# One table of order and one of buffer numbers, made anew for a kernel that mixes a spectral filter and an MLP

## The chip, the cores and the metric

The kernel runs on one core of a Trainium2 chip. The metric is device time in microseconds (us), the median of three runs; less is better. The core has a matrix engine (PE, whose weight loads are shown apart as PEld), a vector engine (DVE), an activation engine (ACT), a general engine (POOL), and SP, which here only issues DMAs. Each engine works through its own row of instructions in order; semaphores tell one engine what another has finished, and also tell an engine of its own results.

## The reference

Two branches are computed from one 2048 x 512 input and mixed by a gate, all in float32:

```python
g = sigmoid((x * gate_w).sum(-1, keepdims=True))
a = irfft2(rfft2(x) * (w_r + 1j * w_i))        # x: 2048 x 512, w: 2048 x 257
b = gelu(x @ w1 + b1) @ w2 + b2                # w1: 512 x 1792, w2: 1792 x 512
out = g * a + (1 - g) * b
```

Both branches read the same x; it reaches the kernel in two layouts, xt and xc.

## The kernel before

The 2048 rows are 16 blocks of 128, numbered j. Matrix products at full precision are made of three products of rounded parts (high x high, high x low, low x high); the parts are made by ACT (the high one, a rounding copy) and by DVE (the low one, a subtraction). Where DVE is to be spared, ACT writes the negated high part and POOL adds the source to it with an accumulating DMA (`acc`, L412).

The spectral branch has four stages. `forward` (L585 on) transforms one block: sums and differences of x (eo, w), products with a cosine table (pd), rounding into zb (L628 by ACT, L632 by DVE), products with a table tf (py), and results in y. `stage1` and `filt` are radix-4 butterflies on DVE (`radix4`, L680 to L688, the products with the filter wf at L775 to L779). `stage4` and `inverse` (L825 on) go back: turned rows sw and pq, products pz with a table tg, rounding into zb (L852 by ACT, L853 by DVE), products pa with ci, sums w, and an accumulating DMA that adds the other branch.

The MLP is worked by groups of hidden features. `seven` makes products of a 2 x 2 block scheme with seven products instead of eight (nuA, uxA, nuB, uxB); `plain` does the first group directly (ph); `gelu` (L919) is applied in place, and `split` makes the parts g_h and g_l (L429 and L476). `down` multiplies with w2: ACT loads the running sum s into a PSUM bank po (L968), PE adds, and ACT copies it back into s (L429). The last group goes through `down_seven` (dx, dm, dn, dz, dl), whose results are the output.

All these steps are collected in a graph of 2146 numbered steps. Nothing plans at build time: `ORDER` (L126) lists all the steps in the order in which they are emitted, and `SLOTS` (L212) gives, for each buffer in the order of first use, its number in a pool: 7 buffers of 2 KB per partition (t2k), 3 tables (ttab), 8 for rounded x (xhl), 46 working buffers (w) and the 8 PSUM banks (ps). Each engine's row is the part of `ORDER` that is its own; SP and POOL issue their DMAs in that order too. A buffer is taken over by another tile when the last reader of the former has been emitted:

```python
last = held.get((b.tag, b.slot))
assert last is b or last is None or last.left == 0
assert last is b or not b.onto or last.full
held[b.tag, b.slot] = b
```

The first step that writes a buffer taken over waits, by semaphore, for the last steps that used it. Where that last step is of the same engine, the engine waits for its own result; so it does where an operation reads, or writes over, what the operation ahead of it on its engine has made or read. PE's matmuls are all issued at L420, so they are told apart by the names of their tiles.

Of the kernel before, what the change touches and what calls it, by code (L numbers as in the profile page):

```python
# [126 lines left out]
0 2 8 15 12 108 6 9 489 1 31 32 60 18 7 19 20 28 27 30 22 21 16 17 490 59 491 13 14 10 29 23 496 62 107 55 3 56 24 58  # L127
497 498 25 36 4 38 86 85 57 64 11 114 63 492 37 40 66 65 39 499 35 46 81 82 111 110 72 84 192 113 42 43 47 112 67 5
500 41 70 68 69 44 197 198 48 199 73 119 219 225 45 200 49 120 83 90 138 224 71 143 145 227 226 118 74 121 144 146 165
123 171 173 170 172 50 51 75 115 87 139 127 91 76 508 124 166 493 549 494 495 167 77 92 94 122 125 516 248 672 520 33  # L130
61 89 626 140 169 168 517 518 566 93 128 512 116 521 129 130 548 126 580 174 96 97 117 501 522 88 34 98 502 175 509
176 513 510 628 95 131 99 132 177 221 142 504 178 179 52 53 100 519 141 503 148 530 133 511 180 78 101 514 181 582 523
147 150 80 505 183 539 54 193 581 152 506 182 220 515 102 194 222 195 103 184 149 542 583 223 540 156 507 565 564 543
527 153 151 185 186 157 154 585 552 196 629 365 595 201 271 541 892 229 202 187 531 544 528 135 249 250 568 550 366
251 553 203 367 252 231 204 188 545 554 584 158 159 532 155 206 524 189 191 571 207 536 569 160 575 546 210 104 587
630 570 106 233 529 230 79 161 205 105 588 586 556 272 525 234 228 547 589 208 232 576 591 572 211 134 235 212 537 538
573 533 590 592 551 676 209 555 254 236 273 275 627 256 602 526 1458 342 274 557 567 294 684 648 258 633 259 561 558
162 634 237 559 534 238 574 317 319 213 604 607 631 650 593 642 594 369 318 632 239 278 214 535 562 608 240 215 635
636 577 276 277 279 677 653 281 609 637 654 603 680 241 253 282 638 560 606 295 644 285 280 598 655 656 782 610 578
685 242 652 673 286 737 388 647 255 368 611 613 296 596 939 411 283 639 287 284 243 678 322 563 321 190 288 679 640  # L140
612 605 257 674 675 686 657 289 649 299 597 260 290 262 614 615 579 320 261 298 618 658 164 263 297 291 622 681 651
616 323 619 343 344 346 645 264 345 617 412 216 265 682 620 683 659 293 687 300 664 623 325 621 266 624 625 660 700
163 267 327 706 668 669 302 670 701 301 328 707 304 245 454 389 390 392 347 303 305 331 665 306 292 661 413 671 307
218 702 391 414 453 662 708 136 600 324 326 244 703 308 456 663 415 329 330 332 348 709 309 704 333 601 334 350 217
710 372 352 694 353 335 310 311 695 705 356 599 312 688 689 374 377 336 784 268 270 785 349 741 351 643 137 455 458
357 459 783 378 337 457 371 358 460 945 789 373 354 690 355 790 313 247 246 646 666 667 787 696 788 793 359 691 394
269 791 724 375 376 338 462 360 361 370 395 697 794 461 692 725 417 379 792 397 400 464 396 398 399 467 416 736 738
698 711 401 468 938 828 726 718 719 380 693 727 393 803 720 893 712 463 743 1462 314 419 465 713 402 425 339 721 739
421 699 730 897 731 795 422 466 315 381 316 426 418 403 362 742 744 745 943 382 740 747 748 786 404 420 714 427 899
900 722 383 405 901 423 894 384 364 732 428 340 801 1459 751 406 715 728 898 903 746 424 385 471 363 407 799 757 836  # L150
386 387 729 436 341 429 430 753 408 410 904 944 1078 485 832 448 431 433 1119 733 758 432 409 723 905 760 798 469 434
734 797 752 478 804 472 477 435 829 806 902 946 470 475 476 735 474 830 759 749 716 762 717 767 809 810 833 763 755
800 449 480 959 840 26 450 764 808 813 765 750 479 486 1463 482 831 768 481 796 473 483 484 487 761 949 774 814 837
834 950 811 838 1084 906 984 641 488 775 1464 776 812 777 895 805 778 1079 766 835 807 820 815 816 779 862 856 1065
1067 769 850 839 824 857 780 1085 781 770 863 851 1064 1109 1107 858 1110 864 852 1070 841 842 821 1066 844 845 825
826 822 827 896 865 843 771 772 823 773 988 846 1071 1069 853 859 817 818 874 875 847 914 860 866 985 916 1105 1087
907 1068 1106 1086 1088 1112 1108 754 908 1432 910 1089 1111 1113 1114 1159 802 1115 819 1116 861 1120 1121 848 919
1122 1123 1124 437 867 947 918 1081 948 886 868 1080 1117 854 1154 1152 109 992 756 1155 1153 880 849 1082 1118 855
869 881 876 923 940 989 990 913 1072 912 887 986 1520 996 993 941 1436 1156 1157 915 917 888 924 925 877 889 870 1434
1433 920 994 1073 1437 911 1090 909 997 930 1083 934 1158 921 926 1125 1669 1126 1127 1164 922 927 928 1165 1128 1091  # L160
929 931 935 932 878 998 942 890 882 960 871 936 1161 1092 937 991 987 951 962 1465 995 883 879 1438 1016 1024 891 872
1129 1093 873 1094 1439 1130 1074 1460 1546 954 965 952 1075 964 884 1017 1451 1440 1442 957 1461 1166 1184 961 1160
438 969 1178 953 1467 966 885 1032 1452 967 1162 1025 1466 968 963 970 1441 976 1163 1201 1202 1477 1478 1000 1167
1026 971 972 933 977 1472 1185 1168 1169 1095 1487 1076 439 1170 973 1179 1181 1180 974 1008 1001 1516 1515 1018 980
981 982 983 1077 1019 1002 1182 1171 1453 999 1468 1187 1479 1033 1009 1027 975 1448 1131 1003 1056 1443 1010 1048
1004 1020 1005 1207 1186 1473 1188 1480 978 1205 1484 1668 958 1040 1132 1189 1519 1550 1057 1011 1134 1133 1021 1034
1028 1029 1199 1200 1183 1049 1135 1203 1012 1469 979 1481 1225 1226 1449 1486 1470 1517 1435 1711 1213 1137 1444 1013
1446 1670 1041 1058 1050 1489 1518 1059 1204 1208 1042 1136 1210 1551 1552 1209 1447 1671 1214 1206 1216 1490 1051
1522 1138 1485 1215 1139 1524 1474 1445 1492 1043 1052 1053 1673 1140 1227 1141 1142 1471 1527 1450 1143 1211 1228
1674 1229 1212 1217 1547 1548 1035 1491 1060 1493 1475 1488 1172 1061 1675 1147 1676 1454 1528 1529 1530 1521 1044  # L170
1482 1045 1230 1219 1554 1144 1145 1036 1037 1526 1523 1218 1150 1455 1677 1495 1678 1679 1220 1222 1680 1531 1231
1232 1500 1525 1496 1533 1497 1456 1681 1494 1498 1502 1146 1534 1535 1151 1476 1503 1221 1173 1536 1504 1505 1712
1532 1499 1537 1538 1234 1672 1683 1685 1501 1684 1549 1553 1507 1223 1682 1457 1483 1713 1555 1294 1558 1539 1540
1688 1506 1508 1689 1509 1690 1687 1541 1511 1542 1233 1149 1692 1693 1512 1513 1148 1174 1543 1175 1096 1587 1691
1235 1236 1556 1514 1099 1694 1686 1707 1699 1592 442 1708 1559 1700 1597 1176 440 1703 1544 1701 1560 443 1557 1224
1510 1177 1100 1190 1237 1194 1192 1702 1695 1598 1704 1567 1593 1705 1709 1696 1577 1545 1191 1706 1568 1714 1561
1594 1599 1569 1588 1582 441 1697 1562 1600 1601 1197 1198 1710 1698 1743 1583 1097 1572 446 1563 1815 1193 1102 1195
1196 1589 1241 1564 1570 1571 1814 1239 1101 1253 1238 1240 1244 1243 1098 1245 1844 1573 447 1246 1247 1248 1584 1879
1242 1325 1103 1254 1595 1578 1596 1574 1739 1565 1579 1719 1744 1566 1880 1715 1881 1590 1249 1591 1735 1585 1816 444
1580 1740 1104 1250 1252 1326 1251 1258 1883 1581 1586 1731 1716 1745 1255 445 1845 955 1575 1736 1717 1884 1323 1257  # L180
1256 1259 1305 1720 1746 1718 1727 1732 1737 1721 1851 1576 1723 1327 1722 1738 1885 1329 1324 1022 1850 1818 1813
1817 1342 1404 1054 1328 1343 1846 1260 1265 1330 1335 451 1062 1336 1046 1261 1887 1966 1063 1332 1262 1875 1331 1733
1728 1006 1741 1742 1333 1263 1853 1724 1353 1820 1297 1822 1014 1400 1334 1276 1401 1405 1888 1847 1402 1729 1730
1268 1030 1856 1876 1857 1403 1824 1829 1409 1407 1819 1858 1725 1825 1821 1264 1877 1406 956 1859 1940 1849 1337 1848
# [1198 lines left out]
```

## Time and profile before

| | |
|---|---|
| median of 3 runs | 358.88 us (358.22 to 358.91) |
| the profiled execution | 358.41 us |
| its span, first to last instruction | 356.6 us |
| mean granted TensorE clock | 0.996 |
| DMA moved | 74.63 MB, mean 209 GB/s |
| chain that ended last, by engine | PE 62%, ACT 17%, DVE 15%, issue 4% |

The span is cut into rows by stage, and each row gives busy time and the number of instructions by engine. Times within the span count from its start. Matmuls are pipelined and their ends are modelled, so PE is best read by how fast one start follows another. A "chain of waits" is followed back from the last instruction: at each step to what released it, or to the instruction ahead of it on its engine. In a row of a timeline the first number is the start, the second the duration (records of one engine overlap), and what stands in brackets is idle time and what ended it.

### The profile page before, as it was taken

The numbers are of one execution on the slowest core, as the hardware profiler recorded it, in microseconds if no ns is written. First come the engines' busy times: TensorE is split into PE (matmuls) and PEld (weight loads), VectorE is DVE, ScalarE is ACT, GpSimd is POOL, SyncE is SP. The second block draws the span as 40 slices with busy tenths as digits, with TensorE's granted clock in tenths as the row PEclk, the third lists the DMA queues.
The fourth block names the chain that finished last, engine by engine and source line by source line (L and its number), as shares of the span: only waits on it lengthen the run. The fifth ranks groups of instructions, "written<-read, shape, count | busy, mean of one in ns | idle before, by whom it ended". The sixth has DMA issues, their size and how long they took to land.

```text
span 356.6 us, 5786 instructions
## 1 busy us (share of the span) xinstructions
PE 348.4 (98%) x1742; PEld 291.6 (82%) x1742; DVE 336.6 (94%) x700; ACT 303.5 (85%) x631; POOL 56.8 (16%) x75
## 2 busy tenths in 40 slices
PE   8999999999999999999999999999999999999894
PEld 7988888888887888888888888887878888888773
DVE  5999999999899999999999999999999999999991
ACT  3999999999999958996968983888999999999632
POOL 1011001100112003020213030000200000443520
PEclk9999999999999999999999999999999999999998
DMA  7999949863899699799899655856755629499996
GB/s 205 389 247 266 361 133 295 199 194 112 254 300 187 114 345 272 157 277 269 267 274 195 167 78 125 283 194 205 153 134 148 210 74 251 68 170 211 162 219 204
DMA packets 47719, 74.63 MB, mean 209 GB/s; under 512 B 5544, under 2 KB 18344, under 8 KB 47688
## 3 DMA queue, kind: packets, MB, share of 16 engines
q1 hardware_dynamic: 37528, 58.42, 50.1%
q0 software_dynamic: 9728, 15.51, 27.5%
q10 hardware_dynamic: 432, 0.33, 0.3%
q8 instruction: 14, 0.23, 0.3%
q14 instruction: 17, 0.14, 0.1%
HBM read 52.02 MB, written 17.31 MB: 194 GB/s over the span
## 4 chain that ended last, share of the span: by engine, by line
PE 62%; ACT 17%; DVE 15%; issue 4%; DVEq 0%; ACTq 0%
PE po L420 21%; PE uxB L420 7%; PE uxA L420 6%; PE nuB L420 5%; PE nuA L420 5%; PE ph L420 4%; PE pd L420 3%; PE dx L420 3%; PE py L420 3%; ACT sw L836 2%; PE pa L420 2%; DVE y L682 1%; DVE y L680 1%; PE none L420 1%; PE pz L420 1%
## 5 line engine op out<-in xcount | busy, mean ns | idle before, releaser
L968 ACT ACTIVATE po<-s 128x512 f32<-128x512 f32 x40 | 23.6, 601 | 4.2 <-DVE g_12l L476 1.7
L429 ACT ACTIVATE s<-po 128x512 f32<-128x512 f32 x40 | 22.9, 591 | 1.7 <-PE po L420 1.5
L836 ACT ACTIVATE sw<-y,keep 64x512 f32<-64x512 f32 x32 | 22.7, 719 | 1.6 <-DVE y L684 1.0
L775 DVE TENSOR_TENSOR m<-y,wf 128x514 f32<-128x514 f32 x32 | 21.3, 690 | 0.7
L420 PE MATMUL py<-zb,tf 128*128 128x258 f32 x96 | 20.9, 300 | 0.1
L420 PEld LDWEIGHTS pz<-tg,pq 128*128 128x128 f32 x128 | 17.5, 190 | 1.7 <-DVE pq L840 0.3
L420 PE MATMUL pz<-tg,pq 128*128 128x128 f32 x128 | 18.8, 275 | 0.0
L420 PEld LDWEIGHTS py<-zb,tf 128*128 128x128 f32 x96 | 16.0, 189 | 3.2 <-ACT pys L648 0.6
L420 PE MATMUL pa<-zb,ci 128*128 128x256 f32 x96 | 17.1, 292 | 1.5 <-DVE zb L853 1.0
L420 PE MATMUL pd<-cf,w 128*128 128x129 f32 x128 | 18.6, 275 | 0.0
L420 PEld LDWEIGHTS pa<-zb,ci 128*128 128x128 f32 x96 | 14.4, 188 | 4.9 <-ACT od L429 1.7
L420 PEld LDWEIGHTS pd<-cf,w 128*128 128x128 f32 x128 | 17.4, 190 | 1.1
L420 PE MATMUL nuB<-xB,wB0h 128*128 128x512 f32 x56 | 17.5, 393 | 0.0
L978 ACT ACTIVATE s<-po,b2t 128x512 f32<-128x512 f32 x16 | 10.8, 694 | 6.9 <-PE po L420 6.7
L420 PE MATMUL nuA<-xA,wA0h 128*128 128x512 f32 x48 | 15.0, 393 | 0.0
L632 DVE TENSOR_TENSOR zb<-pd,zb 128x256 fp32r<-128x256 f32 x32 | 13.3, 419 | 1.5 <-ACT logit L631 1.4
L593 DVE TENSOR_TENSOR eo<-xf 128x256 f32<-128x256 f32 x32 | 12.7, 417 | 1.2 <-DMA xf<-in_x0g 1.0
L652 ACT ACTIVATE y<-pys 64x257 f32<-64x257 f32 x32 | 13.2, 416 | 0.6
L840 DVE TENSOR_TENSOR pq<-y,sw 128x256 f32<-128x256 f32 x32 | 13.1, 417 | 0.4 <-ACT sw L836 0.3
L414 POOL DMA_DIRECT2D wA0l<-in_w x6 | 5.1, 898 | 52.4 <-DVE wsA L1188 23.8
L596 DVE TENSOR_TENSOR w<-eo 128x256 f32<-128x256 f32 x32 | 12.8, 419 | 0.3
L414 POOL DMA_DIRECT2D w<-bacc x8 | 10.9, 1369 | 9.3 <-DVE w L881 3.4
(595 smaller groups left out, 1270.5 us busy)
## 6 DMA issues: line engine op xcount, KB each, us to landing
wf<-in_wf SPq DMA_DIRECT2D x16, 257.0 KB
xf<-in_xt SPq DMA_DIRECT2D x14, 256.0 KB
tf<-tf SPq DMA_DIRECT2D x16, 192.0 KB
wrA<-in_w SPq DMA_DIRECT2D x12, 256.0 KB
xbA<-in_xc SPq DMA_DIRECT2D x8, 256.0 KB
xbB<-in_xc SPq DMA_DIRECT2D x8, 256.0 KB
bacc<-s SPq DMA_DIRECT2D x8, 256.0 KB
w<-bacc POOLq DMA_DIRECT2D x8, 256.0 KB, 4.9
```

The costliest lines, as they stand in the source:

```text
L414: return add("pool", 0.92, 3.3, lambda: nc.gpsimd.dma_start(dst(), src(), accum_op=ALU.add), reads, writes, 2.2 * kb / 350)
L420: pe.matmul(ps, w, x, start=start, stop=stop, **more)
L429: a(lambda: act.activation(o.ap(), i.ap(), AF.Copy, scale=scale), n, [i], [o])
L593: v(lambda s=s, op=op: vec.tensor_tensor(eo.ap()[:, s], x.ap()[:, 0:2], x.ap()[:, 2:4], op=op), 256, [x], [(eo, s)])
L596: v(lambda s=s, op=op: vec.tensor_tensor(w.ap()[:, s], eo.ap()[:, :, 0], eo.ap()[:, :, 1], op=op), 256, [eo], [(w, s)])
L632: v(lambda c=c: vec.tensor_tensor(segs(xl, c), both(c), segs(xh, c), op=ALU.subtract), 256, [ps[c], (xh, c)], [(xl, c)])
L652: a(lambda o=o, i=i: act.activation(Y[j].ap()[o:o + HP, 1], pys.ap()[i:i + HP, 1], AF.Copy), 257, [(pys, 1)], [(Y[j], 1 + k)], more=0.07)
L775: v(lambda mk=mk, k=k, y=y, w=w: vec.tensor_tensor(mk.ap(), y.ap(), w.ap()[:, k:k + 1, :ND].to_broadcast([P, 2, ND]), op=ALU.mult), 514, [ ...
L836: a(lambda sw=sw, y=y, o=o, i=i: act.activation(sw.ap()[o:o + HP], y.ap()[i:i + HP], AF.Copy, scale=keep.ap()[i:i + HP]), 512, [y, keep, * ...
L840: v(lambda sw=sw, pq_=pq_, y=y, k=k, op=op: vec.tensor_tensor(pq_.ap()[:, k], y.ap()[:, k], sw.ap()[:, 1 - k], op=op), 256, [y, TURNED[c], ...
L968: a(lambda ps=ps, n=n, o=o: act.activation(ps.ap(), o.ap()[:, n], AF.Copy), size, [o], [ps], more=0.04)
L978: a(lambda o=o, ps=ps, q=q: act.activation(o.ap(), ps.ap(), AF.Identity, bias=b2t.ap()[:, q:q + 1]), 600, [b2t, ps], [o])
```

## The change

`ORDER` and `SLOTS` are replaced by new lists of the same 2146 steps and of the same buffers. The planner that made the new ones, which is not part of the kernel, counts an engine's wait for its own last result where it takes over a buffer from its preceding operation. No other line changes; the pools keep their sizes. The first lines of both tables:

```diff
 ORDER = """
-0 2 8 15 12 108 6 9 489 1 31 32 60 18 7 19 20 28 27 30 22 21 16 17 490 59 491 13 14 10 29 23 496 62 107 55 3 56 24 58
+0 2 3 19 16 8 9 6 489 496 1 32 31 34 27 12 28 21 20 7 22 490 29 23 30 14 18 15 17 4 56 55 24 60 58 13 57 497 498 25 36
...
 SLOTS = """
-0 0 0 1 2 6 8 0 0 0 0 0 0 4 0 1 1 2 3 0 6 1 0 0 7 0 4 5 7 2 0 10 1 2 0 0 5 0 0 0 1 7 2 4 3 5 4 34 13 0 6 2 3 2 5 7 0 0
+0 0 0 1 2 6 9 0 0 0 0 0 0 4 1 0 0 2 3 0 6 1 0 1 5 1 4 5 4 0 1 0 2 7 2 0 3 0 0 0 0 5 0 5 3 4 2 14 12 2 12 2 3 1 5 3 6 1
...
```

What it moves is shown at three places. The first is DVE's row some 55 rows ahead of its end, in the last group of the MLP (g2 and g3 are values behind the gelu, g5f their parts) and the last inverse transform (zb from pz). Before:

```order
L1238 SCALAR_TENSOR_TENSOR g2_11_3919<-gb_2689,uxB50_3599 128x512 [waits DMAHW3_49,Activation_49]
L490 TENSOR_TENSOR g5f3_3930<-g2_10_3735,g5f2_3902 128x512 [waits DMASW0_49,Activation_49]
L1137 TENSOR_TENSOR g2_10_3735<-g3_11_3828,g2_10_3735 128x512 [waits DVE_49]
L853 TENSOR_TENSOR zb1_106<-pz4_3858,zb0_88 128x4x128 [waits PE_49]
L853 TENSOR_TENSOR zb1_106<-pz0_3822,zb0_88 128x4x128 [waits PE_49,Activation_49]
```

and after the change, in the same part of DVE's row:

```order
L490 TENSOR_TENSOR g5f3_3932<-g2_10_3716,g5f2_3903 128x512 [waits DMAHW2_49,PE_49,Activation_49]
L1238 SCALAR_TENSOR_TENSOR g2_12_3934<-gb_2718,nuB60_3865 128x512 [waits DMAHW1_49,Activation_49]
L840 TENSOR_TENSOR pq8_3908<-y_271,sw8_3850 128x256
L993 TENSOR_TENSOR s31_2804<-s31_2804,y_271 128x512
L853 TENSOR_TENSOR zb1_87<-pz4_3862,zb0_89 128x4x128
L1137 TENSOR_TENSOR g2_10_3716<-g3_11_3831,g2_10_3716 128x512 [waits DVE_49]
```

The L1137 row writes over g2_10, which the L490 row reads. It stood right behind L490; now four rows lie between them, so that the result it waits for is five rows old.

The second place is PE's row at the last inverse transform (pz feeds zb, pa reads zb; dx, dm and uxB are products of the MLP's last group, po of `down`). Before:

```order
L420 MATMUL pz12_3997<-tg01_3577,pq12_3881 128x128 x2
L420 MATMUL pz8_3981<-tg01_3577,pq8_3810 128x128 x2
L420 MATMUL dx1_3990<-gx60_3962,v06_3505 128x512 x3
L420 MATMUL uxB60_3885<-xBt4_2263,wB16_3733 128x512 x6
L420 MATMUL pa01_4052<-zb0_88,ci_3004 128x256 x2
L420 MATMUL pa01_4052<-zb1_106,ci_3004 128x256
```

and after the change:

```order
L420 MATMUL pz12_3990<-tg01_3523,pq12_3798 128x128 x2
L420 MATMUL dx0_4019<-g5f0_3825,v05_3624 128x512
L420 MATMUL dx0_4019<-g5f1_3845,v05_3624 128x512
L420 MATMUL dx0_4019<-g5f0_3825,v05_3624 128x512
L420 MATMUL dm1_4023<-g5f2_3903,vsh5_3657 128x512
L420 MATMUL dm1_4023<-g5f3_3932,vsh5_3657 128x512
L420 MATMUL dm1_4023<-g5f2_3903,vsl5_3755 128x512
L420 MATMUL uxB60_3887<-xBt4_2407,wB16_3518 128x512 x6
L420 MATMUL pa01_4037<-zb0_89,ci_2462 128x256 x2
L420 MATMUL po2_320_3619<-g3_5h_3279,wb5h_2841 128x512
L420 MATMUL po2_320_3619<-g3_5l_3281,wb5h_2841 128x512
L420 MATMUL po2_320_3619<-g3_5h_3279,wb5l_2897 128x512
```

Behind the last row shown three products of dx follow before the first pa that reads zb1, DVE's part. Between the last pz and that pa stood nine products of 512 columns; now there are 18. Further on, the second half of pa01's products, which three products of dx divided from the first, stands behind six products (dx1 and dm0), and three more of dx1 lie inside it.

The third place is the start of SP's row. Before:

```order
L551 DMA b2t<-in_b 128x4
L522 DMA xf_95<-in_xt 128x256
L911 DMA war_97<-in_w 128x256
L522 DMA xf_95<-in_xt 128x256
L911 DMA war_97<-in_w 128x256
```

and after the change:

```order
L522 DMA xf_93<-in_xt 128x256
L911 DMA war_96<-in_w 128x256
L522 DMA xf_93<-in_xt 128x256
L911 DMA war_96<-in_w 128x256
L527 DMA cf<-cf 128x258 x2
```

The load of b2t, the bias of the second layer, was the first of all and stands 23rd now; what stood behind it has moved up by one.

198 rows, old and new, of tables (ORDER, SLOTS) are left out of this document.

## The prediction

> **What bounds the kernel now.** I read the page's busy table first, then the table by stage, then the chain of waits.
>
> ```profile
> PE 348.4 (98%) x1742; PEld 291.6 (82%) x1742; DVE 336.6 (94%) x700; ACT 303.5 (85%) x631; POOL 56.8 (16%) x75
> ```
>
> ```profile
> 20.00:100.00 80.00, 79.86 (x434) 68.07 (x433) 76.01 (x175) 78.75 (x200) 7.96 (x12) 1.00 0.78 225
> 100.00:240.00 140.00, 140.00 (x616) 114.98 (x615) 138.25 (x264) 113.25 (x218) 22.40 (x26) 1.00 0.83 219
> 240.00:330.00 90.00, 89.34 (x491) 75.67 (x490) 87.14 (x180) 86.91 (x151) 16.28 (x18) 1.00 0.66 164
> 330.00:351.30 21.30, 20.27 (x98) 16.36 (x96) 19.29 (x36) 9.97 (x19) 7.47 (x7) 1.00 0.92 206
> ```
>
> In a row by stage the columns are the stage, its length, then busy us (and count) of PE, PEld, DVE, ACT and POOL, the granted clock, the DMA share and GB/s. PE, DVE and ACT all look nearly full, so the share of busy time doesn't decide, and PE's ends are modelled. What decides is how fast PE's matmuls follow each other. The chain of waits shows their price where nothing disturbs them:
>
> ```profile
> 112.32 5.44 PE uxA L420 x24
> ```
>
> ```profile
> 301.99 0.47 PE pa L420 x4
> 302.46 0.89 PE pz L420 x8
> ```
>
> That is 5.44/24 = 0.227 us for 512 columns, 0.47/4 = 0.118 for 256, and 0.89/8 = 0.111 for 128 columns in float32 (two records per matmul). Now each stage can be priced. From 100 to 240 there are 616 matmuls in 140 us, 0.2273 each: PE loses 0.3 us at most. From 240 to 330 the groups by shape are these two, two odd records, and 277 of 512 columns for the rest of the 491:
>
> ```profile
> L420 PE MATMUL pz<-tg,pq 128*128 128x128 f32 x128 | 18.8, 275 | 0.0
> L420 PE MATMUL pa<-zb,ci 128*128 128x256 f32 x84 | 15.0, 291 | 0.5 <-ACT od L429 0.3
> ```
>
> They need 14.3 + 9.9 + 62.8 us, and the stage lasts 90, so 3.1 are lost. From 20 to 100 (255 of 512 columns, 81 of 258, 96 of 129) the same sum leaves 2.0; behind 330 it leaves 1.8, and before 20, beside the 1.1 us until the first matmul, 1.4. **PE's losses are 8.7 us in all** (1.4 + 2.0 + 0.3 + 3.1 + 1.8, rounded). The matmuls, the 1.1 at the head and some 5.3 behind the last matmul stay whatever the order. So an order can win at most 8.7 us, and almost nothing in the middle 140.
>
> **The change, part by part.** It is one table of order and one of buffer numbers; no operation is added or taken away. The sum is made against the profiled execution, 358.41 us (span 356.6 and 1.8 around it), which lies 0.47 under the median of 358.88.
>
> *Term 1: waits for the engine's own last result.* Here are neighbours on DVE, then on ACT, with and without such a wait:
>
> ```profile
> 317.64 0.68 DVE L1238 SCALAR_TENSOR_TENSOR g<-gb,uxB 128x512 f32<-128x512 f32 x1
> 318.24 0.68 DVE L490 TENSOR_TENSOR g5f<-g,g5f 128x512 fp32r<-128x512 f32 x1
> 318.96 0.69 DVE L1137 TENSOR_TENSOR g<-g,g 128x512 f32<-128x512 f32 x1
> ```
>
> ```profile
> 290.30 0.57 ACT L429 ACTIVATE s<-po 128x512 f32<-128x512 f32 x1
> 290.90 0.60 ACT L968 ACTIVATE po<-s 128x512 f32<-128x512 f32 x1
> 291.44 0.55 ACT L429 ACTIVATE uxB<-nuB 128x512 f32<-128x512 f32 x1
> 291.92 0.59 ACT L429 ACTIVATE od<-pa 128x512 f32<-128x512 f32 x1
> ```
>
> The L490 row follows its predecessor after 0.60 us. The L1137 row overwrites g, which L490 has just read, waits for it, and starts 0.72 after it: **the wait costs 0.12 us**. On ACT the copy of po into s is followed by the load of po from s after 0.60, while uxB<-nuB, as large a copy from PSUM without such a wait behind it, is followed after 0.48: again 0.12. Counted over the two orders, rows that wait for the row right ahead fall from 72 to 33 on DVE and from 44 to 31 on ACT. By stage, before and after: DVE 15 and 5 in 20 to 100, 39 and 21 in 100 to 240, 12 and 2 in 240 to 330; ACT 5 and 0, 30 and 21, 7 and 7. (The few others are at the two ends.) What goes in the middle is worth nothing: PE loses nothing there, and DVE, busy for 138.25 of 140 us, is fast enough beside it. In the two stages where PE does lose time, (10 + 5) x 0.12 = 1.8 us and 10 x 0.12 = 1.2 us go, beside losses of 2.0 and 3.1. Between nothing and all 3.0 can reach PE. I take half, **-1.5**, since the waits for which PE's weight loads stand end with ACT as often as with DVE, and most of what goes is DVE's:
>
> ```profile
> PEld pa L420 <- ACT od L429: 1.7, 4, 0.5
> PEld pa L420 <- DVE zb L853: 1.2, 1, 1.2
> ...
> PEld uxB L420 <- ACT uxB L429: 0.6, 1, 0.6
> PEld py L420 <- ACT pys L648: 0.6, 1, 0.6
> ```
>
> A rule of the Trainium skill speaks against this term: "VectorE: DVE Perf Modes", section "The DRAIN you can't avoid", has eight copies in a row take as long with a semaphore after each as with one behind the last, and says "the semaphore costs nothing extra here". By it term 1 would be 0 and the sum 1.5 us higher. The trace disagrees, with 0.72 beside 0.60.
>
> *Term 2: the last inverse transform.* The longest single loss stands near the end of PE's row:
>
> ```profile
> 328.05 0.89 PE pz L420 x8
> 328.94 0.70 PE dx L420 x3
> 329.64 1.40 PE uxB L420 x6
> 331.04 0.04 DVEq L490
> 331.07 1.16 DVE zb L853 x2
> 332.23 0.04 issue
> 332.27 0.74 PE pa L420 x4
> 333.02 0.69 PE dx L420 x3
> 333.71 0.98 PE pa L420 x6
> ```
>
> ```profile
> 329.53 1.07 ACT L852 ACTIVATE zb<-pz 128x512 fp32r<-128x512 f32 x2
> ```
>
> After the last pz at 328.94 ACT must round two blocks into zb and DVE must form two remainders, which end near 332.2. PE has only dx, uxB and two of pa in between, 0.70 + 1.40 + 0.24 us, so it could go on at 331.25 and goes on at 332.27: 1.0 us lost. The next six pa take 0.98 where 6 x 0.118 = 0.71 would do: 0.27 more. In the new order dx, dm, six uxB, two of pa, three of po and three of dx stand there, 18 x 0.227 + 0.24 = 4.3 us instead of 2.3, and six matmuls, 1.4 us, divide the second half of pa, where three did. DVE's two zb keep their place, 32 rows ahead of its last. The cover exceeds the lateness twice over, so I take all of it, **-1.3**; it is 0 only if DVE itself gets 2 us later against PE, and term 1 makes it earlier.
>
> *Term 3: the head.* b2t, not needed before the first sums are evicted, leaves the first place in SP's row; the loads behind it are issued one place earlier.
>
> ```profile
> 0.75 0.39 SPq L551 DMA_DIRECT2D b2t<-in_b  x1
> 1.20 0.42 SPq L522 DMA_DIRECT2D xf<-in_xt  x1
> ```
>
> ```profile
> 5.14 1.06 PE L420 MATMUL ph<-xf,war 128*128 128x128 f32 x4
> 5.96 0.37 PE L420 MATMUL none<-zero 128*128 128x256 f32 x1
> 6.27 1.58 PE L420 MATMUL ph<-xf,war 128*128 128x128 f32 x12
> ```
>
> The four ph records at 5.14 need 0.45 us and the next real ones start at 6.27, with the second half of war, so up to 0.45 us (1.20 - 0.75) can be won. The transfers share their engines, and xf of ACT's queue now has an earlier rival: it may win nothing or lose as much. I take **-0.2**.
>
> *Term 4: new places.* Every matmul has new neighbours, and some result will come late where none did. The longest of the waits for ACT quoted above are 0.5 and 0.6 us in one piece, the 1.7 us of pa are four of 0.4 on average; between none and four such may appear. I take two small ones, **+0.7**; the largest gap of before, the 1.0 of term 2, bounds a single one.
>
> Sum: -1.5 - 1.3 - 0.2 + 0.7 = -2.3, so 356.1 on the profiled execution's scale. Set half-way from its scale to the median's, that is **356.3 us**.
>
> **Rivals.**
>
> *1: the freed time isn't PE's.* DVE and ACT start earlier and then wait for what PE makes. For it: PE waits for a single result at each place, and an engine that is ahead gains nothing. Against it: DVE and ACT are busy for 76.01 and 78.75 of 80 us, then 87.14 and 86.91 of 90, just where PE loses. Term 1 is then 0: 356.3 + 1.5 = 357.8. (The rule of the Trainium skill weighed under term 1, from "VectorE: DVE Perf Modes", would give the same time; the spacing of 0.72 speaks against it, and it adds nothing to this chance.)
>
> *2: slower, by the first group's accumulated halves.* The low halves of wA go through POOL, in order, once ACT has written their negated copies:
>
> ```profile
> 29.50 0.84 POOL L414 DMA_DIRECT2D wA0l<-in_w  x1 [7.83 <-ACT zb L628]
> ```
>
> ```profile
> wA0l<-in_w POOLq DMA_DIRECT2D x6, 256.0 KB, 5.8
> ```
>
> ```profile
> 41.53 0.39 PE L420 MATMUL nuA<-xA,wA0l 128*128 128x512 f32 x1
> ```
>
> Issued at 29.50 and landed some 5.8 us later, this half has 6.2 us in hand before nuA reads it at 41.53. In the new order ACT makes that copy 2.7 us of its own work later and PE comes to the matmul 0.8 us of its work earlier: 2.7 are left. ACT is the fullest engine of that stage (78.75 of 80 us), so lateness there isn't made up. It decides as soon as the copy comes over 2.7 us later than the order implies. One that misses by as much as POOL waited for ACT at this very place, 7.83, costs 7.83 - 2.7 = 5.1 us, and DVE and ACT behind it don't win it back: 356.3 + 5.1 = 361.4; a miss of half that gives 357.5. Against it: the raw blocks from which these halves are made stand earlier in SP's row, 18th and 19th rather than 27th and 30th.
>
> That the table doesn't do what it says can be left out, since the counts of waits above are of the two programs.
>
> **How the numbers follow.** Forecast 0.58, its own range 354.0 to 358.0 (term 1 whole and no term 4 give 353.9; term 1 at a quarter and term 4 doubled give 358.1). Rival 1 has 0.20, rival 2 0.22. A measurement of this kernel tells 0.2%, 0.72 us, from no change, so faster is below 358.16. The forecast lies there but for 0.02, and of rival 1, at 357.8, some 0.12: with 0.01 of rival 2, **0.68 faster**. Of rival 1 0.06, of rival 2 0.05 and of the forecast 0.02 are the same: **0.13**. Slower: 0.16 of rival 2, 0.02 of rival 1 and 0.01 of the forecast, **0.19**. The range is 354.0 to 359.8, which leaves out the lower edge of the forecast and some 0.15 of rival 2.
>
> **What would show it.** The spacing of DVE's rows should be 0.60 at the places named, with few of 0.72, and DVE's busy share lower by about 1%. PE's row should show pa without a gap at the last inverse, and some 490 matmuls in less than 90 us in the stage from 240 on. The first real ph should stand before 6.2. Rival 1 would show DVE and ACT idle more, with PE's losses as before; rival 2 a pause of over 1 us in PE's row before the first nuA, ended by a DMA. A loss of over 1 us at any place that I don't name would break term 4, and with it the forecast.

## The result and the profile after

The changed kernel takes **353.64 us** (353.41 to 353.74, 4 runs) beside 358.89 for the kernel before: ratio 0.9854, 95% interval 0.9837 to 0.9871, or 5.2 us. 356.3 was forecast, with 354.0 as the lower end: the direction was right, the size half of what came. The profiled execution took 353.74 us, its span is 352.0.

The busy table of the changed kernel, and its table by stage (columns as in the prediction):

```profile
PE 344.8 (98%) x1742; PEld 291.9 (83%) x1742; DVE 333.4 (95%) x700; ACT 301.6 (86%) x631; POOL 56.6 (16%) x75
```

```profile
20.00:100.00 80.00, 79.98 (x435) 68.36 (x435) 77.01 (x176) 78.71 (x202) 7.97 (x12) 1.00 0.78 228
100.00:240.00 140.00, 140.00 (x618) 115.28 (x617) 137.55 (x267) 113.21 (x219) 22.44 (x26) 1.00 0.83 223
240.00:330.00 90.00, 90.00 (x504) 78.21 (x503) 88.56 (x184) 87.74 (x155) 19.40 (x20) 1.00 0.68 160
330.00:351.30 21.30, 16.38 (x80) 13.51 (x78) 14.15 (x26) 6.95 (x14) 4.12 (x4) 0.97 0.87 218
```

Shares of busy time say almost nothing here; counts do. From 240 to 330 PE now runs 504 matmuls instead of 491. The chain of waits, which gave PE 62% before, is PE's own row:

```profile
PE 96%; DVE 1%; DMA 1%; issue 0%; ACT 0%; DVEq 0%
```

PE's losses, worked out as in the prediction (start to start, less 0.227, 0.1175 or 0.1115 us by shape), and of them the waits longer than 0.095 us in one piece (each cell and each sum rounded by itself):

| stage | loss before | loss after | long waits before | after |
|---|---|---|---|---|
| 0 to 20 | 1.4 | 1.1 | 1.2 | 1.0 |
| 20 to 100 | 2.0 | 1.5 | 0.9 | 0.3 |
| 100 to 240 | 0.4 | 0.1 | 0.2 | 0.1 |
| 240 to 330 | 3.1 | 0.9 | 2.1 | 0 |
| from 330 | 1.8 | 0.1 | 1.7 | 0 |
| sum | 8.6 | 3.7 | 6.0 | 1.4 |

PE loses 4.9 us less, and 4.7 of that are long waits that are gone, 3.7 of them behind 240. In the list of what PE's weight loads wait for, the stage from 240 to 330 has seven rows before and none after. The last inverse transform in PE's row of the changed kernel, and DVE's two zb that it needs:

```profile
326.18 0.40 PE L420 MATMUL pa<-zb,ci 128*128 128x256 f32 x2
326.42 0.40 PE L420 MATMUL po<-g_5h,wb5h 128*128 128x512 f32 x1
...
327.12 0.85 PE L420 MATMUL dx<-gx,v 128*128 128x512 f32 x3
327.81 0.63 PE L420 MATMUL pa<-zb,ci 128*128 128x256 f32 x4
```

```profile
325.38 1.28 DVE L853 TENSOR_TENSOR zb<-pz,zb 128x512 fp32r<-128x512 f32 x2
```

The zb end at 326.66, 1.15 us ahead of the pa that reads them; none of these rows of PE has idle time in brackets. And DVE's row in the last group; before, L1137 started 0.72 behind the row whose result it waited for:

```profile
318.63 0.70 DVE L1231 TENSOR_TENSOR uxB<-uxB,fiveB 128x512 f32<-128x512 f32 x1 [0.29 <-PE uxB L420]
319.24 0.68 DVE L1137 TENSOR_TENSOR g<-g,g 128x512 f32<-128x512 f32 x1
319.84 0.68 DVE L490 TENSOR_TENSOR gx<-g,gx 128x512 fp32r<-128x512 f32 x1
320.44 0.68 DVE L1238 SCALAR_TENSOR_TENSOR g<-gb,uxB 128x512 f32<-128x512 f32 x1
```

Every start follows the last by 0.60 or 0.61, and DVE now waits for PE.

### The profile page after: what moved, and what is told of

The parts are those of the page before. It is cut to its first block, busy times and chain, and to the rows that moved or that the text cites. A ratio compares the mean times of both kernels' runs of the same rounds, so it can differ in the third digit from the quotient of the medians.

```text
span 352.0 us, 5796 instructions
## 1 busy us (share of the span) xinstructions
PE 344.8 (98%) x1742; PEld 291.9 (83%) x1742; DVE 333.4 (95%) x700; ACT 301.6 (86%) x631; POOL 56.6 (16%) x75
## 4 chain that ended last, share of the span: by engine, by line
PE 96%; DVE 1%; DMA 1%; issue 0%; ACT 0%; DVEq 0%
PE po L420 37%; PE uxB L420 11%; PE uxA L420 9%; PE nuB L420 8%; PE nuA L420 7%; PE pd L420 4%; PE pz L420 4%; PE py L420 3%; PE pa L420 3%; PE ph L420 3%; PE dx L420 3%; DMA xf<-in_x0g 1%; PE dm L420 1%; PE dn L420 1%; PE dz L420 1%; DVE eo L593 0%
## 5 line engine op out<-in xcount | busy, mean ns | idle before, releaser
L628 ACT ACTIVATE zb<-pd 128x256 fp32r<-128x256 f32 x32 | 12.1, 392 | 0.4 <-PE pd L420 0.4
L420 PEld LDWEIGHTS nuB<-xB,wB0h 128*128 128x128 f32 x56 | 10.4, 188 | 2.0
```

What stands on the lines that cost most here:

```text
L420: pe.matmul(ps, w, x, start=start, stop=stop, **more)
L628: a(lambda c=c: act.activation(segs(xh, c), both(c), AF.Copy), 256, [ps[c]], [(xh, c)])
```

## The experiments

Two things changed at once: how often DVE and ACT wait for their own last result (72 to 33 rows on DVE, 44 to 31 on ACT), and the order. Buffer numbers alone move the first without the second. Each run was compared with runs of the kernel before on the same chip (358.1 to 358.5 there). Where a table was set in other lines, L851 stands for L853 and so on.

### Buffer numbers alone

`s_all` and `s_mid`: before's order, new numbers. Of 900 numbers 374 and 175 differ; the first of s_all:

```diff
 SLOTS = """
...
-34 13 0 6 2 3 2 5 7 0 0 14
+23 13 0 6 2 3 2 5 7 0 1 14
...
```

> The kernel before with its own order of steps, row for row, and buffer numbers changed alone: two numbers change places wherever a step of DVE or ACT would take over a buffer from the step right ahead of it. Rows that wait for the row right ahead fall from 72 to 33 on DVE and from 44 to 33 on ACT, nearly the counts of the changed kernel (33 and 31). Theory 'own waits, by stage' (term 1 of the prediction): 10 + 4 such waits of 0.12 us go in each of the two stages where PE loses or fewer, half of them reach PE: about -1.1 us, 357.8. Theory 'own waits, carried': also the 20 + 7 that go between 100 and 240 count, since DVE and ACT come out of that stage earlier and PE's later losses (3.1 us behind 240) shrink: -2.5 us or more, 356.4 or less. Theory 'order': buffer numbers alone win nothing, 358.7 or more.

> As the run before this one, but the buffer numbers change places only where DVE's row stands between 100 and 240 us: there DVE's waits for the row right ahead fall from 39 to 19, ACT's from 30 to 23, elsewhere nothing changes. Theory 'own waits, by stage': 0, since PE loses nothing in that stage, 358.9. Theory 'own waits, carried': -1 us or more, 357.9 or less, and PE's losses shrink behind 240, not before. Theory 'order': 358.9.

Measured: 366.09 (ratio 1.0235, 1.0197 to 1.0274) and 367.83 (1.0261, 1.0233 to 1.0288). No theory had this. The timelines of ACT and DVE of s_mid show why:

```profile
147.02 0.60 ACT L429 ACTIVATE g_10h<-nuA 128x512 fp32r<-128x512 f32 x1 [4.35 <-DMA su<-wAsh]
149.07 0.21 ACT L772 ACTIVATE wf<-edges 128x4 f32<-128x4 f32 x1 [1.46 <-DMA wf<-in_wf]
```

```profile
149.31 0.70 DVE L775 TENSOR_TENSOR m<-y,wf 128x514 f32<-128x514 f32 x1 [5.38 <-ACT wf L772]
```

g_10h had been given a buffer that a store (su<-wAsh) was still reading, and ACT stood for 4.35 us. In s_all the same wait took 6.9 us. A number that saves 0.12 us on DVE can cost some 36 times that at a DMA, or more. These two runs say nothing of the waits themselves.

`a_all` and `a_mid`: the changed kernel's order, with own waits put back by buffer numbers (357 and 207 differ; no stall by a DMA came with them).

```diff
 SLOTS = """
...
-1 0 1 5 1 4 5 4 0 1 0 2 7 2
+0 0 0 5 1 4 5 4 1 0 0 2 7 2
...
```

> The changed kernel with its own order of steps, row for row, and buffer numbers changed alone, so that DVE and ACT again take over buffers from the step right ahead: waits for the row right ahead rise from 33 to 72 on DVE (as before the change) and from 31 to 41 on ACT. Theory 'own waits, by stage': 10 + 0 come back in 20 to 100 and 7 + 2 in 240 to 330, half of 2.3 us reaches PE: 354.8. Theory 'own waits, carried': +2.5 us or more, 356.1 or more. Theory 'order': at most +0.3, 353.9.

> As the run before this one, but only between 100 and 240 us: DVE's waits for the row right ahead rise from 22 to 38 there, ACT's from 21 to 29. Theory 'own waits, by stage': 353.6, no change against the changed kernel. Theory 'own waits, carried': 354.6 or more, with the new losses behind 240. Theory 'order': 353.6.

Measured: **354.45** (0.9888, 0.9873 to 0.9903) and **353.52** (0.9862, 0.9843 to 0.9880). 39 waits on DVE and 10 on ACT, 5.9 us of their rows, cost 0.8 us by the medians and 1.2 by the ratios; the 16 and 8 in the middle cost nothing. Compared row by row with the changed kernel, DVE in a_mid is up to 1.3 us late, at 200, and 0.4 at 240, while PE's row keeps its times from 60 us to the end. In this order the theory "carried" falls, and with a_all it is seen that the order alone, with as many own waits on DVE as before, brings 4.1 of the 5.2 us.

`s2_all`, `s4`, `s4_mid`: before's order again, with numbers that touch no load or store soon before or after.

> The kernel before with its own order and buffer numbers changed alone, as in s_all, but two numbers change places only where the buffer that is given up isn't taken by a load or an accumulating DMA within the next 120 steps, nor by another engine within 20. Rows that wait for the row right ahead fall from 72 to 38 on DVE and from 44 to 38 on ACT. If s_all was slower by what its buffers did to loads, this one isn't. Theory 'own waits, by stage': half of (6 + 4 + 4) x 0.12 us, -0.8, 358.1. Theory 'own waits, carried' or 'DVE's lag': DVE reaches 331 some 4 us of its own work earlier and the gap there closes, -1.2 to -2.5, 356.4 to 357.7. Theory 'order': 358.6 or above.

Measured: 357.41 (0.9972, 0.9953 to 0.9992), with two waits of DVE for DMAs left, 2.1 and 2.0 us, at 63 and 119. The next two are free of them (174 and 165 numbers differ):

```diff
 SLOTS = """
...
-5 32 24 41 0 0 0 3 2 1
+5 32 24 36 0 0 0 3 2 1
...
```

> The kernel before with its own order and buffer numbers changed alone, behind 100 us only, and only where the buffer given up isn't wanted by a load within 300 steps, and the one taken was last used by no DMA within 200: so free of the two stalls by DMAs (2.0 us each) that s2_all had. Waits for the row right ahead: 47 instead of 72 on DVE, 38 instead of 44 on ACT. Theory 'DVE's lag': 25 x 0.12 = 3.0 us less on DVE's row, of which PE gets back 2 or more: 356.5 or less. Theory 'own waits, by stage' (term 1): half of (3 + 4) x 0.12, -0.4, 358.0. Theory 'places': 358.4.

> As s4, but only where DVE's row stands between 100 and 240 us: 19 waits fewer there on DVE, 2 on ACT, 2.3 us of DVE's row. Theory 'DVE's lag': -1.5 to -2.3 us, 356.2 to 357.0, all of it behind 240. Theory 'own waits, by stage' (the middle is worth nothing) and theory 'places': 358.4.

Measured: **355.50** (0.9935, 0.9917 to 0.9952) and **356.80** (0.9964, 0.9952 to 0.9975). The middle stage, where PE loses nothing, is worth 1.3 us; six further waits on DVE and four on ACT behind 240, 1.2 us of their rows, are worth 1.3 more. The table by stage of s4 from 240 on:

```profile
240.00:330.00 90.00, 89.15 (x495) 76.89 (x494) 87.15 (x182) 87.77 (x154) 18.12 (x19) 1.00 0.69 165
```

495 matmuls instead of 491, and PE's loss behind 240 is 2.7 instead of 4.9. So in before's order the theory "carried" holds: what DVE is late by at 240 is paid behind it. The same rows in before and in s4_mid show it, near 240 and near 270 (DVE, then PE). Before:

```profile
242.81 0.47 DVE L820 SCALAR_TENSOR_TENSOR ownx<-ownx,al,ownz 4x256 f32<-4x256 f32 x1
270.98 0.69 DVE L682 TENSOR_TENSOR y<-d0d,d0d 128x512 f32<-128x512 f32 x1
241.68 0.62 PE L420 MATMUL nuB<-xB,wB0h 128*128 128x512 f32 x2
269.64 1.05 PE L420 MATMUL pz<-tg,pq 128*128 128x128 f32 x8
```

and in s4_mid:

```profile
241.17 0.47 DVE L820 SCALAR_TENSOR_TENSOR ownx<-ownx,al,ownz 4x256 f32<-4x256 f32 x1
269.81 0.69 DVE L682 TENSOR_TENSOR y<-d0d,d0d 128x512 f32<-128x512 f32 x1
241.64 0.62 PE L420 MATMUL nuB<-xB,wB0h 128*128 128x512 f32 x2
268.47 1.05 PE L420 MATMUL pz<-tg,pq 128*128 128x128 f32 x8
```

At 240 DVE is 1.64 us ahead of before's times and PE 0.04; at 270 both are 1.17 ahead, and at the end of PE's row it is still 1.1. The two orders differ: the waits are worth 2.6 us in the one and 0.8 in the other.

### Rows moved at PE's largest gaps, and DVE's load changed

`b_od` moves three steps of before's ORDER by one row each, `b_t2` four steps, `b_od_t2` all seven (in the diffs 1285, 1314 and 1622 are od<-pa; 1799 the pa that reads zb1; 2086 dx0; 2114 and 2115 dm1; 2087 dm0):

```diff
 ORDER = """
...
-1415 1285 1286
+1285 1415 1286
...
-1382 1314 1315
+1314 1382 1315
...
-1750 1622 1996
+1622 1750 1996
...
```

```diff
 ORDER = """
...
-2016 1799 2086 1991
+2016 2086 2114 1799 1991
...
-1800 1801 1802 2114 2087 1778
+1800 2087 2115 1801 1802 1778
...
-2058 2115 1806
+2058 1806
...
```

> The kernel before with three steps moved and nothing else: in three of the eight inverse transforms ACT's copy od<-pa goes one row forward, ahead of a row (ownz, sw, sw) that stood between the last pa it reads and itself. There PE lost 0.32, 0.41 and 0.56 us (at 267.7, 276.6 and 300.8), each a wait for that copy and a further 0.10 on the matmul behind it. Theory 'order' (the late stage's losses come from where a copy stands in ACT's row, not from waits for the own last result): -1.3 us, 357.6 (on 358.9). Theory 'DVE's lag' (DVE, late by its own waits, only meets PE at the next place): the gap at 331, where PE waits for DVE's zb, grows by what is won, and the time stays at 358.6 or above.

> The kernel before with four steps moved and nothing else: at the last inverse transform six matmuls (dx0 and dm1) go ahead of the pa01 that waits for DVE's zb, and six (dm0, dm1) between its two halves, as the changed kernel has it. Term 2 of the prediction alone: -1.3 us (the gap of 1.0 to 1.2 at 331 and 0.27 behind it), 357.6. If what is won there is lost again at the next wait before the end: 358.6 or above.

> Both of the edits above. Theory 'order': they add, -2.6 us, 356.3. Theory 'DVE's lag': the covers of the second are spent on the gain of the first, -1.5 us, 357.4.

Measured: 358.64 (1.0012, 0.9999 to 1.0025), 358.97 (1.0017, 1.0001 to 1.0033), 359.53 (1.0034, 1.0017 to 1.0050). None gained. The gaps went where they were meant to and came back further on. What PE's weight loads wait for from 240 on, in b_od and in b_t2 (total, times, longest):

```profile
PEld pa L418 <- DVE zb L851: 1.6, 2, 1.3
PEld po L418 <- ACT po L966: 0.9, 2, 0.5
...
PEld pa L418 <- ACT u L427: 0.5, 1, 0.5
PEld pa L418 <- ACT zb L850: 0.4, 2, 0.3
PEld pa L418 <- ACT od L427: 0.4, 1, 0.4
```

```profile
PEld dx L418 <- DVE dz L1062: 1.4, 1, 1.4
PEld pa L418 <- ACT od L427: 1.3, 3, 0.5
PEld dm L418 <- DVE zb L851: 0.7, 1, 0.7
PEld dx L418 <- DVE dn L1062: 0.5, 1, 0.5
```

In b_od the waits for od fell from 1.7 to 0.4 us, and those for po, u and zb took their place. In b_t2 the 1.2 for zb became 0.7 for zb, 0.5 for dn and 1.4 for dz: the moved matmuls had been the cover of later rows of DVE. PE was waiting for engines that were late at several rows, not for one row.

`b_less` and `a_all_x4` change DVE's load instead:

```diff
-            less(b00, b01, b00)
+            less(b00, b01, b00, 64 if s == "B" else 512)
...
```

```diff
-                v(lambda mk=mk, k=k, y=y, w=w: vec.tensor_tensor(
-                    mk.ap(), y.ap(), w.ap()[:, k:k + 1, :ND].to_broadcast([P, 2, ND]), op=ALU.mult), 514, [y, w], [mk])
+                v(lambda mk=mk, k=k, y=y, w=w, q1=q1: [vec.tensor_tensor(
+                    mk.ap(), y.ap(), w.ap()[:, k:k + 1, :ND].to_broadcast([P, 2, ND]), op=ALU.mult)
+                    for _ in range(2 if q0 == 0 and q1 < 2 else 1)], 514, [y, w], [mk])
```

> The kernel before with eight of DVE's subtractions xbB<-xbB,xbB (between 112 and 194 us) narrowed from 512 columns to 64, all waits and rows as they were; the second half's block forms of x are then left unfinished, so the output differs. DVE gets some 8 x 0.45 = 3.6 us less to do, in a stage where PE loses nothing. Theory 'DVE's lag' (from 100 us on DVE's row never idles; what it is behind there is paid by PE behind 240): -2.5 us or more, about 355.5, with PE's losses behind 240 down from 4.9 to under 2.5. Theory 'places' (each loss behind 240 comes from the order around it): 358.5, no change.

> The run a_all (the changed kernel's order with 39 waits put back on DVE, 354.45) with four of DVE's products m<-y,wf between 123 and 160 us made twice, into the same buffer: 4 x (0.60 + 0.12) = 2.9 us more on DVE's row. Theory 'DVE's lag': a_all's waits had used up what the new order left DVE to spare, so this comes out at the end: +2 us or more, 356.5 or above. Theory 'places': the middle stage is worth nothing to PE, 354.5.

Measured: 357.02 (0.9969, 0.9955 to 0.9984), that is -1.1 where -2.5 or more was expected, and 356.99 (0.9969, 0.9957 to 0.9980), that is 2.5 us over a_all (2.9 by the ratios). Behind the narrowed rows the next starts after 0.135 us instead of 0.60, so DVE had 3.7 us less to do in the middle. At 180 its row is 2.1 us ahead of before's, but at 240 only 1.2: it waits in between, 0.6 us at the longest for ACT's g_8h, where before's DVE had no wait over 0.15 from 150 to 240. PE is 0.3 ahead at 240, 1.2 at 270, and no more after. So a lead of 1.2 us at 240 was worth 1.2 us; what a greater one would bring isn't shown. The remaining 3.9 us of PE's loss behind 240 arise there.

In a_all_x4 the 2.9 us weren't carried: PE loses 2.7 us between 100 and 240, where it lost 0.1 in a_all, and behind 240 only 0.3 more. The longest piece stands right behind the doubled rows:

```profile
159.01 1.20 PE L420 MATMUL uxA<-xAt,wA 128*128 128x512 f32 x4 [0.96 <-DVE nuA L1232]
```

So in a_all the waits put back had taken what DVE had to spare in the middle, and more work there costs PE time at once.

### Both at once, and the head

> s4's buffer numbers (25 waits fewer on DVE, 6 on ACT, behind 100 us) and b_t2's four moved steps at the last inverse transform. Theory 'both are needed' (rows moved pay only when DVE isn't behind): s4 (355.5) less the gap of 0.7 + 0.1 at 329 and 0.27 behind it: 354.5. Theory 'a third cause': as s4, 355.5, the gap turning up further on as in b_t2.

> s4's buffer numbers and b_od's three steps, ACT's copy od<-pa one row forward in three inverse transforms. In s4 PE still lost 0.30 + 0.10 and 0.33 + 0.10 at two of them. Theory 'both are needed': 355.5 - 0.8 = 354.7. Theory 'a third cause': 355.5, with the gap at 329 grown.

> s4's buffer numbers with the moved steps of both b_od and b_t2, seven of 2146. Theory 'both are needed': 355.5 - 1.0 - 0.8 = 353.7, as fast as the changed kernel. Theory 'a third cause': 355 or above.

Measured: 356.02 (0.9929, 0.9906 to 0.9952), 355.37 (0.9906, 0.9887 to 0.9925), 356.38 (0.9932, 0.9912 to 0.9951), beside 355.50 for s4 alone. "Both are needed" falls too: with s4's numbers the waits for dz (1.3 us) and dn are there again as soon as the four steps are moved. For od's three rows the times alone don't decide, since the interval of s4_od overlaps that of s4 and its ratio lies 1.0 us lower; but PE's loss behind 240 is 2.7 us in both (3.4 and 3.5 in s4_t2 and s4_od_t2).

`b_b2t` moves one step:

```diff
 ORDER = """
-0 2 8 15 12 108 6 9
+0 2 8 15 12 6 9
...
-61 89 626 140
+61 89 108 626 140
...
```

> The kernel before with one step moved: the load of b2t from the first place of SP's row to the 23rd. Term 3 of the prediction: -0.2 us, 358.2, with up to 0.45 at the most. If the head isn't set by SP's row: 358.4.

Measured: 357.76 (0.9980, 0.9968 to 0.9992): -0.3 to -1.1 us. Its profile shows 0.2 of that at the head; the rest lies within what runs of before's order differ by.

### The two orders crossed

`h_ab` takes the first 1960 steps of the changed order and then what is left in before's; `h_ba` takes 2000 of before's, then what is left in the changed one. Their seams, the first against the changed table, the second against before's:

```diff
 ORDER = """
...
-1930 1666 2040 1975 1978 1959 1660 2027 1755
+1930 1666 2040 1785 1784 2083 1660 1959 2027
...
```

```diff
 ORDER = """
...
-1931 2034 1765 1766 2044 1786 1987
+1931 2034 1765 2072 2074 1793 2038
...
```

> The first 1960 steps of the changed kernel's order with its buffer numbers (to about 310 us), then what is left in the order of before, with before's buffer numbers carried over: its PE row at the last inverse transform, its DVE, ACT and SP rows there. Theory 'the last stage's order': the gaps of before at 331 come back, 353.6 + 1.0 or more, 354.6 or above. Theory 'DVE ahead' (the same rows cost nothing once DVE comes into them early): 353.9 or less.

> The first 2000 steps of before's order with s4's buffer numbers (to about 323 us), then what is left in the changed kernel's order, all engines together. Theory 'the last stage's order': s4's gaps behind 320 (0.9 + 0.3) go, 355.5 - 1.0 = 354.5 or less. Theory 'DVE ahead': DVE comes into the last stage as late as in s4, so 355.3 or above, with the gap at another row.

Measured: 356.93 (0.9960, 0.9948 to 0.9973) and 357.27 (0.9971, 0.9955 to 0.9987). Both lose at the seam, which blurs them: in h_ab PE waits 2.2 us in one piece for DVE's g at 317, in h_ba 0.85 for od at 324. So h_ab tells little. In h_ba PE's weight loads wait for these from 320 on, the first of the two od at the seam:

```profile
PEld pa L418 <- ACT od L427: 1.6, 2, 0.9
PEld pa L418 <- DVE zb L851: 1.1, 1, 1.1
PEld dx L418 <- DVE dz L1062: 0.2, 1, 0.2
```

Behind the seam stand the changed kernel's own last rows, which wait for nothing there, and h_ba is 1.8 us slower than s4 (1.3 by the ratios). So these rows aren't free whatever comes ahead of them. It doesn't prove "DVE ahead", since DVE's lateness at zb is in part the seam's own: at 324.96, 5 us ahead of zb, it had stood 1.13 us for ACT's uxB.

## Why the forecast was half of it

With term 1 whole and no term 4 the prediction's own sum was 353.9, beside 353.64 measured. That it comes so near is luck, since most of what the forecast missed came with the order and not with term 1.

**The table of losses** was right as a sum, 8.7 us, but only 6.0 were long waits. The other 2.7 were not there to be won: most of it is a nanosecond or so per matmul that the rounded prices leave, and the new order has 2.3 of it too (see also the last section). Of the 6.0 the change won 4.7; behind 20 us it won 4.5 of 4.9. No step of the prediction allowed for that.

**Term 4, the step that failed most**: away from the two places of terms 2 and 3 the new order was entered as a cost alone, +0.7. All that the prediction gave to the order is -1.3 - 0.2 + 0.7 = -0.8, and a_all, the new order with as many own waits on DVE as before, brings -4.1. PE's loss from 240 to 330, 3.1 before and 0.9 after, is 1.2 there: 1.9 of that stage's 2.2 us come with the order. The sign of the term itself wasn't wrong, since a few results do come late in new places: uxA at 52 (0.18 us, and 0.11 on the matmul behind it), and at the head pd for DVE's cf, counted under term 3. What was missing is a term for the waits that the new order ends at places not named.

**Term 1, the other step that failed**: "What goes in the middle is worth nothing: PE loses nothing there". The price of a wait, 0.12 us, was right, and so were the counts. But in before's order the middle's waits were worth 1.3 us (s4_mid), since DVE carries its lateness into the next stage, and those behind 240 were worth all of their 1.2 us (s4 beside s4_mid), where half was taken. In the changed order the middle's are indeed worth nothing (a_mid), and all of them together 0.8 (a_all), because there DVE has time to spare. A price per stage, taken from losses of the same stage, could not show either. The stage from 240 to 330 was put at -0.6 (half of 1.2) and gave -2.2; from 20 to 100 -0.9 was put and -0.5 came.

The rule of the Trainium skill that was weighed beside it ("VectorE: DVE Perf Modes", section "The DRAIN you can't avoid": the semaphore costs nothing extra) would have given 0 for this term. s4 differs from before by buffer numbers alone and is 2.6 us faster; the measurement decides.

**Term 2**: the gap at 331 went, with 0.4 more than the -1.3 forecast. But the reason given, 18 products of cover in place of nine, doesn't carry it: much the same rows moved alone (b_t2, with 15) win nothing, and in h_ba they wait for zb again. The exception that the prediction allowed, DVE 2 us later against PE, isn't what came. In b_t2 the cover was taken from later rows of DVE, dn and dz. Cover is worth something when DVE comes in time for the next rows as well.

**Term 3**: -0.2 forecast; 0.3 less loss before 20 us, and b_b2t gained. The first real ph stands at 5.80 instead of 6.27, but pd then waits 0.52 for DVE's cf.

**Rival 1** (the freed time isn't PE's) describes the changed order (a_mid) and not the kernel before. **Rival 2** didn't come: no pause stands ahead of the first nuA. Of the signs that were named, DVE's spacing of 0.60, pa without a gap and ph before 6.2 came. DVE's busy time fell by 1%, but its share of the shorter span rose from 94% to 95%, and 504 matmuls, not some 490, stand from 240 to 330.

**What both buy, and what stays open**: buffer numbers alone bring 2.6 us, the order alone 4.1, both 5.2, so they overlap. The traces show at the eight inverse transforms what is bought. Each has 12 pa; the third is the first that reads DVE's zb, and the seventh writes to the bank that ACT's copy od has just read. This is how far ahead of that pa the row it needs had ended (us, the eight in order of time; at 0.05 PE had waited for it):

| | DVE's zb | ACT's od |
|---|---|---|
| before | 0.19, 0.66, 0.92, 0.59, 0.22, 1.11, 3.58, 0.05 | 0.05, 0.05, 0.55, 0.35, 0.05, 0.33, 0.22, 0.05 |
| s4 | 0.48, 0.66, 0.88, 0.67, 0.22, 1.11, 3.93, 0.05 | 0.13, 0.05, 0.51, 0.49, 0.05, 0.46, 0.57, 0.05 |
| a_all | 0.46, 0.34, 0.28, 0.65, 0.36, 0.50, 1.10, 0.40 | 0.45, 0.15, 0.05, 0.74, 0.55, 0.38, 0.91, 0.05 |
| after | 1.30, 1.11, 0.89, 1.23, 0.95, 0.95, 1.22, 1.15 | 1.20, 0.80, 0.63, 1.12, 0.81, 0.55, 0.96, 0.59 |

The new order spreads the time ahead evenly over the eight, 0.55 us or more, where before's has up to 3.58 at one and nothing at others. The own waits put back in a_all take up to 0.8 of it, and mostly there is enough left. Which of its moves bring this about was not pinned to a place. One candidate wasn't tried by itself: DVE's waits for ACT between 70 and 100. Before:

```profile
82.06 0.42 DVE L632 TENSOR_TENSOR zb<-pd,zb 128x256 fp32r<-128x256 f32 x1 [0.62 <-ACT logit L631]
94.62 0.43 DVE L649 SCALAR_TENSOR_TENSOR pys<-pys,y 128x257 f32<-128x257 f32 x1 [0.37 <-ACT y L648]
97.39 0.43 DVE L649 SCALAR_TENSOR_TENSOR pys<-pys,y 128x257 f32<-128x257 f32 x1 [0.54 <-ACT y L648]
```

With two more (0.36 at 73.8, 0.31 at 98.7) that is 2.2 us; in the changed kernel there is one such wait behind 70, 0.40 at 88. That DVE enters the middle 1.8 us to the good by this isn't shown, and by b_less a lead of that kind can explain a part only.

## What to carry to other kernels

A stage in which the bounding engine loses nothing may still be where its later losses are made: ask of each engine beside it how far ahead it is when the stage ends, and price what is removed by that. Gaps of the bounding engine behind late engines aren't a sum of places: moving the rows around one gap handed it to the next row that needed one of these engines. When a whole order is new, look for what it ends everywhere, not only at the places that are easy to see. And in giving out buffers, taking the one just released costs an engine 0.12 us, taking one from a DMA in flight cost 2 to 7 here: loads and stores come first.

## What the runs showed of the hardware

Of DVE's rows right behind one of 128 x 512, those that wait for an own result nearly all start either 0.60 to 0.61 us after it (43 before, 55 after, as most rows without such a wait do) or 0.71 to 0.73 (27 before, 10 after). So the wait costs 0.12 us or nothing; in the rows under term 1 the 0.12 was paid for the result of the row right ahead.

PE's row has pieces of 0.075 to 0.095 us over the usual spacing at matmuls for which it shows no wait: 56 before and 52 after, 4.8 and 4.5 us in all. They are no loss. All but four before and one after stand right behind a start that is as much early, at the change from a matmul of 128 or 129 columns to a longer one; these make up for 4.4 and 4.2 us. A matmul right behind one that waited, on the other hand, mostly starts a further 0.10 to 0.11 us late with nothing to make up for it.

The kernel before spread from 357.4 to 360.3 us over all calls, the changed one from 353.4 to 353.7 in four. In several profiles on before's order a product stood still for a load at 183 us, as here in b_b2t; in none on the changed order, nor in the five with s4's numbers:

```profile
183.43 0.50 PE L418 MATMUL nuB<-xB,wB0l 128*128 128x512 f32 x1 [0.71 <-DMA wB0l<-su]
```
